# Declaring a 64-byte mask tile ahead of seven buffer groups of a two-layer attention and Fourier kernel

## The chip, the core and the metric

The kernel runs on one core of one Trainium2 chip. The metric is the device time of one execution in microseconds (us). Before the change it was 1702.32 us, the median of three runs (1701.19 to 1706.34).

## The reference

Four blocks are applied one after the other to an activation of 2048 rows by 640 columns in float32. Each block normalises its input, works on it and adds the result to it.

```python
x = x + _A_ref(_layernorm(x, axis=-1), A_wqkv, A_wo)
x = x + _B_ref(_layernorm(x, axis=-1), B_dft_seq_re, B_dft_seq_im, B_dft_hid_re, B_dft_hid_im)
x = x + _A_ref(_layernorm(x, axis=-1), A_wqkv, A_wo)
x = x + _B_ref(_layernorm(x, axis=-1), B_dft_seq_re, B_dft_seq_im, B_dft_hid_re, B_dft_hid_im)
```

Block A is local attention: 32 heads of 20 columns, and each row attends to itself and to the rows 2, 4, ... 14 above it (8 in all). Rows above the first are masked with -1e9, which is all that the mask tile of this document is for. Block B multiplies the activation by a 640 by 640 and by a 2048 by 2048 discrete Fourier matrix and keeps the real part.

## The kernel before

All matrix products run on TensorE. Each float32 operand is split into a high and a low part, held in the type float32r, and a product is three matmuls (high by high, low by high, high by low: `PASSES`, line 237). A matmul has a stationary operand of 128 by 128 that is loaded into the array (LDWEIGHTS, the rows of PEld), and a moving operand of 128 rows by up to 512 columns that streams past it. In the names of a matmul's row, `m<-r,s`, the moving operand comes first behind the arrow, and the stationary one second.

The work on TensorE, in order, is the following.

- Line 125: 18 warm-up matmuls of zeros in bfloat16, out of the tile `zero`, which has the tag s3.
- Line 381 (`qkv_mm`, block A): the projection to queries, keys and values, 128 groups of 15 matmuls with 480 moving columns. The moving operand is the split weight of one quarter of the heads, in r1_0, r1_1, r1_2 or r1_3; the stationary one is the transposed activation in s0 to s3.
- Line 531 (`wo_mm`, block A): the output projection with 320 moving columns from r2a.
- Lines 346 and 354 (`pc_pe`, `pc_sub`): transposes of 128 by 128 with the identity as the moving operand, and matmuls of 128 to 512 columns that subtract the high part again, with the negated identity `nident` as the stationary operand.
- Line 1004 (`z_mm`, block B): the first part of the sequence transform, 512 moving columns from s0 to s3 and e0 to e2, accumulated over 16 steps.
- Line 1148 (`product`, block B): the rest of the sequence transform, 512 moving columns of a split tile that rotates over zo0, zo1, e0, stg, zo2, e1, stg, ot (and pr2, pr3 in the second block B, line 1205).
- Line 1393 (`hid_mm`, block B): the hidden transform, 320 moving columns from r2a, r1_2, r1_3, pr0 to pr3 and zo3.

The attention itself (lines 450 to 511) runs on VectorE and GpSimd out of the five buffers of the tag win, which are loaded by DMA. ScalarE evicts and splits. The order of the instructions on every engine is written out by hand (a table of steps and phases, lines 868 to 902) or follows the order of the program; no queue in it depends on where a buffer lies.

Where a buffer lies in SBUF follows from the order in which the tags are first declared. The pool `sb` gives each tag, on each of the 128 partitions, as many bytes as its widest tile needs, rounded up to a multiple of 32, and puts the tags one behind the other. Lines 118 to 121 fix that order for the first of them: `zero` claims s3, and the loop of line 119 declares six more tags without using them. The mask follows with 11 float32 numbers, 44 bytes, which take 64. It is written by three memsets on GpSimd (lines 127 to 129) and read twice, each time by one copy of 11 columns to PSUM at the start of a block A (line 872).

In the built program the buffers lie as follows (bytes from the start of a partition; the remainder is that of the start divided by 256).

| buffers, in order | start before | remainder before |
|---|---|---|
| ident, nident, mhalf | 1184, 1696, 2208 | 160, 160, 160 |
| s3 | 2240 | 192 |
| r1_0 | 7360 | 192 |
| pr0 | 27840 | 192 |
| e0, e1, e2 | 32960, 38080, 43200 | 192, 192, 192 |
| win, five buffers of 3520 bytes | 48320 to 62400 | 192, 128, 64, 0, 192 |
| mask | 65920 | 128 |
| pr1, pr2, pr3, r1_1, r2a, r1_2, r1_3, zo2, zo3, ot, s0, s1, stg, zo0, s2, zo1, qs, xa, lg, xr | 65984 to 226752 | 192 each |

All slices that TensorE reads begin a multiple of 256 bytes behind the start of their buffer, so that every matmul operand has the remainder of its buffer. All tiles end at 229312 bytes.

Of the kernel before, what the change touches and what calls it, by code (L numbers as in the profile page):

```python
# [26 lines left out]
P = 128  # L27
# [55 lines left out]
SLOTS = NJ + W - 1  # L83
# [5 lines left out]
def tile_layers(ctx: ExitStack, tc: tile.TileContext, x, wqkv, wo, cs, wre, wim, out):  # L89
# [10 lines left out]
    def nm(base):  # L100
        uid[0] += 1
        return f"{base}_{uid[0]}"

    def T(shape, tag, dt=F32, bufs=1, pool=None):
        return (pool or sb).tile(shape, dt, tag=tag, name=nm(tag), bufs=bufs)
# [9 lines left out]
    nident = T([P, P], "nident", F32R)  # L115
    nc.scalar.activation(nident, ident, AF.Copy, scale=-1.0)
    mhalf = T([P, 4], "mhalf")
    zero = T([P, D], "s3", mybir.dt.bfloat16)
    for tag, w in (("r1_0", D), ("pr0", D), ("e0", 2 * D), ("e1", 2 * D), ("e2", 2 * D), ("win", SLOTS * FE)):
        T([P, w], tag, bufs=NWIN if tag == "win" else 1)  # L120
    mask = T([P, SLOTS], "mask")
    nc.vector.memset(zero, 0.0)
    wb = pt([P, 512], "m1")
    for i in range(NWARM):
# [1438 lines left out]
```

## Time and profile before

| | |
|---|---|
| median of 3 runs (lowest, highest) | 1702.32 us (1701.19, 1706.34) |
| span of the profiled execution | 1700.9 us |
| granted TensorE clock, all through | 1.00 |
| TensorE (PE) busy | 1679.7 us (99%), 8558 matmuls |
| VectorE (DVE) busy | 1339.2 us (79%) |
| ScalarE (ACT) busy | 794.0 us (47%) |
| GpSimd (POOL) busy | 625.8 us (37%) |
| DMA, share of the 16 engines in the main queue | 75.7% |

The profiled execution took 1700.9 us from its first to its last instruction; the profile lists no other time of its own for it. Busy time of TensorE is the union of its matmuls, and each of these is shown with the time that it needs to drain, so a matmul of 512 columns is listed with 389 ns while the next one begins 227 ns behind it. What a matmul costs in a stream is therefore read from the distance between starts, as the chain of waits gives it: there a piece "1.36 PE m L1148 x6" is six matmuls that took 1.36 us from the first start to the start of what follows. That chain is the work that ended last, followed back from the last instruction to what released it.

### The profile page before, as it was taken

What the parts mean: (1) busy time and instruction counts of PE and PEld (TensorE: products, weight loads), DVE (VectorE), ACT (ScalarE), POOL (GpSimd) and SP (SyncE); (2) the same over time, 40 slices, a digit from 0 to 9 for tenths busy, and PEclk for the clock granted to TensorE, in tenths of its full rate; (3) what the DMA queues carried; (4) which work ended last, traced back from release to release, by engine and by line L of the source; (5) the groups of instructions that cost most, each with busy time, mean ns of one, the idle gap of its engine ahead of it and who ended that gap; (6) DMA issues with size and microseconds to landing.
All of it is one profiled execution on the core that took longest, in us unless ns stands there. A gap on an engine that the chain in (4) does not pass through costs nothing.

```text
span 1700.9 us, 25512 instructions
## 1 busy us (share of the span) xinstructions
PE 1679.7 (99%) x8558; PEld 1464.6 (86%) x8558; DVE 1339.2 (79%) x2034; ACT 794.0 (47%) x1617; POOL 625.8 (37%) x588
## 2 busy tenths in 40 slices
PE   9999999989999999999999999999999999999999
PEld 7888988868888887899988889988888888888999
DVE  6999999978588786788639999999784656657784
ACT  5664644544354443536554335444444544444231
POOL 4899999950000000000028988999400000000000
PEclk9999999999999999999999999999999999999999
DMA  8996668857899989986377866788666776787942
GB/s 295 315 322 227 221 227 307 271 206 265 287 370 322 370 270 354 351 331 225 122 226 239 270 217 204 246 284 295 212 234 208 225 228 215 242 282 270 362 164 93
DMA packets 263139, 441.13 MB, mean 259 GB/s; under 512 B 21824, under 2 KB 126016, under 8 KB 260704
## 3 DMA queue, kind: packets, MB, share of 16 engines
q1 hardware_dynamic: 259808, 437.55, 75.7%
q10 hardware_dynamic: 3200, 1.97, 0.4%
q8 instruction: 67, 1.10, 0.3%
q14 instruction: 64, 0.52, 0.1%
HBM read 319.75 MB, written 119.67 MB: 258 GB/s over the span
## 4 chain that ended last, share of the span: by engine, by line
PE 76%; DVE 10%; POOL 6%; DMA 4%; issue 2%; ACT 0%; SPq 0%; DVEq 0%; POOLq 0%; ACTq 0%
PE m L381 19%; PE t L1148 7%; PE aux L1148 7%; PE m L1148 7%; PE pq L1148 5%; PE xt L1148 5%; PE m L1393 4%; PE aux L1393 4%; PE m L1004 3%; PE t L1004 3%; DVE pr L450 2%; PE aux L531 2%; DVE pr L490 2%; POOL pr L509 2%; PE xt L1393 2%
## 5 line engine op out<-in xcount | busy, mean ns | idle before, releaser
L381 PE MATMUL m<-r,s 128*128 128x480 f32 x1920 | 434.5, 381 | 0.6 <-ACT stg L388 0.4
L381 PEld LDWEIGHTS m<-r,s 128*128 128x128 f32 x1920 | 355.4, 188 | 53.5 <-ACT stg L388 0.8
L193 POOL TENSOR_TENSOR stats<-stats,mhalf 128x1 f32<-128x1 f32 (+1 forms) x40 | 29.2, 730 | 512.2 <-ACT stats L189 503.8
L509 POOL TENSOR_TENSOR pr<-pr 128x640 f32<-128x640 f32 x126 | 207.8, 1650 | 23.1 <-DVE pr L490 21.7
L450 DVE TENSOR_TENSOR pr<-pq,win 128x1280 f32<-128x1280 f32 x128 | 189.9, 1484 | 13.8 <-DMA win<-kvb 7.8
L490 DVE TENSOR_TENSOR pr<-pq,win 128x1280 f32<-128x1280 f32 x128 | 190.3, 1487 | 3.7 <-POOL zo L511 1.2
L453 POOL TENSOR_TENSOR pr<-pr 128x640 f32<-128x640 f32 x115 | 164.9, 1434 | 11.2 <-DVE pr L450 11.2
L460 DVE TENSOR_REDUCE lg<-pr 128x64 f32<-128x640 f32 (+1 forms) x128 | 112.7, 881 | 8.0 <-POOL pr L453 7.9
L510 POOL TENSOR_TENSOR pr<-pr 128x320 f32<-128x320 f32 x126 | 112.0, 889 | 9.9
L388 ACT COPY stg<-m 128x480 f32<-128x480 f32 x128 | 71.0, 555 | 92.9 <-PE m L381 69.1
L1004 PE MATMUL m<-s,r 128*128 128x512 f32 x366 | 111.2, 392 | 1.6 <-DMA s<-c0b 1.3
L1004 PE MATMUL t<-s,r 128*128 128x512 f32 x366 | 110.3, 390 | 0.0
L531 PE MATMUL aux<-r2a,ot 128*128 128x320 f32 x540 | 84.7, 310 | 0.7 <-ACT s L369 0.7
L531 PEld LDWEIGHTS aux<-r2a,ot 128*128 128x128 f32 x540 | 81.1, 188 | 2.8 <-ACT s L369 1.2
L1004 PEld LDWEIGHTS m<-s,r 128*128 128x128 f32 x366 | 67.6, 188 | 16.1 <-DMA s<-c0b 1.9
L1004 PEld LDWEIGHTS t<-s,r 128*128 128x128 f32 x366 | 68.7, 188 | 14.5
L1137 ACT CAST zo<-win 128x512 fp32r<-128x512 f32 x76 | 47.2, 621 | 65.4 <-PE xt L1148 30.0
L423 ACT COPY pq<-qs 128x320 f32<-128x320 f32 x64 | 27.5, 430 | 106.0 <-DVE pr L490 73.4
L1138 DVE TENSOR_TENSOR zo<-win,zo 128x512 fp32r<-128x512 f32 x76 | 52.1, 688 | 23.7 <-ACT zo L1137 23.3
L511 POOL TENSOR_TENSOR zo<-pr 128x160 f32<-128x160 f32 x126 | 67.1, 532 | 9.9
L1004 PE MATMUL xt<-s,r 128*128 128x512 f32 x183 | 68.6, 389 | 0.0
L468 ACT ACTIVATE lg<-lg 128x128 f32<-128x128 f32 x64 | 20.3, 317 | 74.6 <-DVE lg L479 74.4
(531 smaller groups left out, 3650.2 us busy)
## 6 DMA issues: line engine op xcount, KB each, us to landing
win<-cs_in SPq DMA_DIRECT2D x192, 256.0 KB, 3.8
win<-kvb SPq DMA_DIRECT2D x96, 440.0 KB, 5.3
win<-kvb SPq DMA_DIRECT2D x64, 360.0 KB, 5.0
kvb<-stg SPq DMA_DIRECT2D x60, 320.0 KB, 4.9
xa<-cs_in SPq DMA_DIRECT2D x66, 256.0 KB, 3.6
e<-cs_in SPq DMA_DIRECT2D x64, 256.0 KB, 3.9
r<-zb SPq DMA_DIRECT2D x12, 1280.0 KB, 5.9
win<-tb SPq DMA_DIRECT2D x56, 256.0 KB, 4.4
```

The source lines that it names most:

```text
L381: nc.tensor.matmul(mt[g][:, : 3 * F], st[:, a, k], wq[q][:, b, k], start=n == 0, stop=n == 14)
L388: nc.scalar.copy(sgs[q][:, :, j % 2], mt.pop(g)[:, : 3 * F].rearrange("p (a f) -> p a f", f=FE))
L450: nc.vector.tensor_tensor(pr, q, wview(u, jp, 0, [[1, FE]]), op=ALU.mult)
L453: nc.gpsimd.tensor_tensor(pv[:, :, 0:10], pv[:, :, 0:10], pv[:, :, 10:20], op=ALU.add)
L460: nc.vector.tensor_reduce(lgs[u][:, :, 2 * jp : 2 * jp + 2].rearrange("p h j w -> p (j w) h"), prq.pop((u, jp)), axis=AX.X, op=ALU.add,)
L490: nc.vector.tensor_tensor(pr.rearrange("p j w (h d) -> p j w h d", d=DH), lgs[u][:, :, 2 * jp : 2 * jp + 2].rearrange("p h j w -> p j w h" ...
L509: g.tensor_tensor(pr[:, :, 0:4], pr[:, :, 0:4], pr[:, :, 4:8], op=ALU.add)
L510: g.tensor_tensor(pr[:, :, 0:2], pr[:, :, 0:2], pr[:, :, 2:4], op=ALU.add)
L531: nc.tensor.matmul(m[:, :320], oT[(c, j)][:, a, k], wo_s["w"][:, b, k, e * 320 : (e + 1) * 320], start=(i, k) == (0, 0), stop=(i, k) == (2 ...
L1004: self.last = nc.tensor.matmul(self.z[t][k], self.xn[c][:, a, j, k * P : (k + 1) * P], self.ct[s][:, b], start=s == 0 and i == 0, stop=s = ...
L1148: nc.tensor.matmul(bank, w(a, kb), hl[b], start=start and (a, b) == (0, 0), stop=stop and (a, b) == (1, 0), skip_group_check=True,)
L1393: nc.tensor.matmul(bank[:, :320], s[:, a, k], w[:, b], start=start and (k, a, b) == (0, 0, 0), stop=stop and (k, a, b) == (KD - 1, 1, 0), ...
```

## The change

The line that declares the mask moves ahead of the first group, to directly behind `mhalf`.

```diff
     mhalf = T([P, 4], "mhalf")
+    mask = T([P, SLOTS], "mask")
     zero = T([P, D], "s3", mybir.dt.bfloat16)
     for tag, w in (("r1_0", D), ("pr0", D), ("e0", 2 * D), ("e1", 2 * D), ("e2", 2 * D), ("win", SLOTS * FE)):
         T([P, w], tag, bufs=NWIN if tag == "win" else 1)
-    mask = T([P, SLOTS], "mask")
     nc.vector.memset(zero, 0.0)
```

No instruction is added, removed or moved: the order on ScalarE and SyncE is the same word for word, and the differences on the other engines are the numbers in the names of two tiles. This is the difference on GpSimd at the start of the program, where the mask is written (with the number that a tile got when it was declared):

```order
 L126 MEMSET mhalf_73 128x4
-L127 MEMSET mask_81 128x11
+L127 MEMSET mask_74 128x11
 masks.py:199 ISA
 masks.py:199 AFFINE_SELECT ident_66<-ident_66 128x128
-L128 MEMSET mask_81 2x3
-L129 MEMSET mask_81 1x4
+L128 MEMSET mask_74 2x3
+L129 MEMSET mask_74 1x4
 L193 TENSOR_TENSOR stats_204<-stats_204,mhalf_73 128x1
```

The mask has become the 74th tile instead of the 81st, and its memsets stand where they stood. On TensorE the 18 warm-up matmuls show `s_6_75` in place of `s_5_74`, and nothing else differs.

What differs is the place of seven tags, each 64 bytes further up, and of the mask:

| buffers | start after | remainder after |
|---|---|---|
| mask | 2240 | 192 |
| s3 | 2304 | 0 |
| r1_0 | 7424 | 0 |
| pr0 | 27904 | 0 |
| e0, e1, e2 | 33024, 38144, 43264 | 0, 0, 0 |
| win, five buffers | 48384 to 62464 | 0, 192, 128, 64, 0 |

From pr1 on everything lies where it lay. In the built program 1641 of the 8558 matmuls read their moving operand from one of the six buffers s3, r1_0, pr0, e0, e1 and e2 (18 in the warm-up, 480 in line 381, 420 in line 1004, 615 in line 1148, 96 in line 1393 and 12 in line 354), 1721 read their stationary operand from one of them, and 330 read both from them. In 2702 matmuls one operand has moved and the other has not.

## The prediction

> **What bounds the kernel now.** I read the page's head first, then the waits of TensorE, then the chain of waits, stage by stage.
>
> ```profile
> span 1700.9 us, 25512 instructions
> PE 1679.7 (99%) x8558; PEld 1464.6 (86%) x8558; DVE 1339.2 (79%) x2034; ACT 794.0 (47%) x1617; POOL 625.8 (37%) x588
> PEclk9999999999999999999999999999999999999999
> ```
>
> TensorE is busy for 1679.7 of 1700.9 us at the full granted clock, so 21.2 us are all that waits can give back. The waits of TensorE, longest first and last of 23 rows, say the same:
>
> ```profile
> PE m L1004 <- ACT r L933: 2.1, 1, 2.1
> PE aux L354 <- ACT s L350: 2.0, 3, 0.9
> ...
> PE m L1004 <- DMA s<-c0b: 1.3, 2, 0.9
> ...
> PE xt L1148 <- DVE s L1311: 0.2, 1, 0.2
> ```
>
> None is over 2.1 us, and DMA has 1.3 us among them. So the time is the sum of what 8558 matmuls cost from one start to the next, and these spacings stand in the chain, where it follows TensorE without a break:
>
> ```profile
> 17.82 34.67 PE m L381 x160
> 739.56 4.40 PE t L1393 x30
> 1300.80 1.36 PE aux L1148 x6
> ```
>
> That is 34.67/160 = 216.7 ns for 480 columns, 4.40/30 = 146.7 ns for 320 and 1.36/6 = 226.7 ns for 512. From 320 to 512 columns the price rises by 80.0 ns for 192 columns, 0.417 ns each (2.4 columns per ns). What is left over is a constant: 226.7 - 213.3 = 13.3 ns for 512 columns, and 146.7 - 133.3 = 13.3 ns for 320. For 480 it is 216.7 - 200.0 = 16.7 ns. This constant is the one thing that a start address could change, because every float32r moving operand outside the transposes begins at remainder 192 today.
>
> Two stages differ in what lies close behind TensorE:
>
> ```profile
> core 0: us, PE busy (x) PEld busy (x) DVE busy (x) ACT busy (x) POOL busy (x), PEclk, DMA share, GB/s
> 100.00:200.00 100.00, 100.00 (x526) 88.75 (x525) 96.47 (x133) 60.48 (x155) 95.45 (x90) 1.00 0.75 247
> 1400.00:1500.00 100.00, 100.00 (x443) 82.81 (x442) 59.96 (x93) 43.82 (x72) 0.00 (x0) 1.00 0.75 249
> ```
>
> In block A (first row) VectorE is busy for 96.47 of 100 us and GpSimd for 95.45, so a faster TensorE would meet them at once. In block B (second row) nothing else is over 83%.
>
> **The change part by part.**
>
> *Declaration.* It adds, removes and moves no instruction and no wait; no queue is passed. The mask's three memsets and two copies of 11 columns read and write another address, and do so at two places in the whole program. Cost 0.
>
> *VectorE and ScalarE, on win and the rest.* The five win buffers rotate from the remainders 192, 128, 64, 0, 192 to 0, 192, 128, 64, 0. If the remainder mattered to these engines, reads out of win would spread wider than reads out of xa, whose two buffers both lie at 192. The views of lines 1137 and 1138, by operand (count, then minimum, median and maximum in ns):
>
> ```profile
> L1137 ACT CAST zo<-win x76: 605/622/630, 423.0 to 1564.2; 128x512 fp32r<-128x512 f32 x76
> L1137 ACT CAST zo<-xa x29: 607/622/631, 374.2 to 1553.1; 128x512 fp32r<-128x512 f32 x29
> L1138 DVE TENSOR_TENSOR zo<-win,zo x76: 679/688/694, 424.0 to 1566.2; 128x512 fp32r<-128x512 f32 x76
> L1138 DVE TENSOR_TENSOR zo<-xa,zo x29: 680/685/693, 375.7 to 1556.1; 128x512 fp32r<-128x512 f32 x29
> ```
>
> Four remainders and one give the same 622 ns and the same spread on ScalarE, and on VectorE the medians differ by 3 ns inside a spread of 15. I take 0. The outer bound is 3 ns for each of VectorE's 2034 instructions, 6.1 us either way, and they lie beside TensorE's work.
>
> *DMA.* The loads of 256 KB, 2048 bytes in a row on a partition, by where they go:
>
> ```profile
> win<-cs_in SPq DMA_DIRECT2D x192, 256.0 KB, 3.8
> xa<-cs_in SPq DMA_DIRECT2D x66, 256.0 KB, 3.6
> e<-cs_in SPq DMA_DIRECT2D x64, 256.0 KB, 3.9
> ```
>
> win, with four remainders, lands in 3.8 us, between xa and e (3.6 and 3.9 us, both at 192). Whatever a transfer gains or loses, TensorE has 1.3 us of waits for DMA to win. Bounds -1.3 to +1.3 us; I take 0.
>
> *TensorE.* 1641 matmuls get a moving operand at remainder 0 instead of 192. 18 of them are the warm-up, which leaves 1623 of float32r: 480 of 480 columns (the quarter of line 381 that uses r1_0), 1035 of 512, 96 of 320 and 12 in line 354. If the whole constant went, that would be 1623 x 13.3 = 21.6 us, and 23.2 us with the extra 3.3 ns for the 480. In the other direction, 2702 matmuls get operands of unequal remainder. Where the trace shows such a matmul already, it pays nothing for it: the subtractions of line 354 stream s at 192 past nident at 160.
>
> ```profile
> 56.29 0.23 PE xt L354
> 56.52 0.06 PE t L354
> 56.58 6.55 PE m L381 x30
> ```
>
> These are 512 and 128 columns. From 56.29 to 56.58 they take 0.29 us; 640 columns at 0.417 ns and two constants of 13.3 ns make 293 ns. So the constant is the same with unequal remainders, at least for 32 bytes of difference.
>
> Does the constant come from the remainder? The warm-up is the only other type in the trace, at the same remainder 192, out of s3:
>
> ```profile
> 4.10 2.32 PE L125 MATMUL m<-s 128*128 128x512 bf16 x10
> L125 PE MATMUL m<-s x10: 379/379/380, 4.1 to 6.0; 128*128 128x512 bf16 x10
> ```
>
> Ten matmuls of 512 columns take 2.32 us, of which the last one's duration is 0.379; (2.32 - 0.379)/9 = 215.7 ns, a constant of 2.4 ns. So remainder 192 as such does not cost 13.3 ns. The other 10.9 ns come with an operand of four bytes, either whatever its address is, or because at twice the bytes the fetch has no slack for a start in the middle of a block. The trace can't tell the two apart, since it holds no stream of long float32r matmuls at another remainder. I take the first, 0, because of the misfit of the 480 columns: a constant that came from blocks of a fixed address grid would be the same for all three lengths, which all start at 192 and are multiples of 128 bytes, yet 480 columns pay 3.3 ns more.
>
> The Trainium skill, SBUF — State Buffer, section "Specifications (TRN2)", gives 16 bytes as the line in SBUF at which an access pays for crossing; 192 and 0 are both multiples of 16, so by this rule the change gives 0, which speaks against it. No run here shows the size of that line; the rows of ScalarE above agree that steps of 64 bytes don't matter. The Trainium skill, TensorE: Matmul & The Clock Gate, section "Back-to-back issue gap", has N/2.4 + 2.5 ns for a warm matmul: the warm-up's 215.7 ns agrees with it, the 226.7 ns of float32r doesn't. If remainder 0 brought the float32r matmuls down to that formula, the change would be worth an estimated 1623 x 10.8 = 17.5 us.
>
> The sum is 0 + 0 + 0 + 0, and the profiled execution stays at 1700.9 us. It lies 1.4 us below the median of the three runs, so I forecast the median, 1702.3 us.
>
> **The rivals.**
>
> *A, faster: TensorE fetches moving operands in 128-byte blocks on a fixed grid.* Starting 64 bytes into a block, 512 columns touch 17 blocks and 320 touch 11; at 13.33 ns a block (32 columns) that is 226.7 and 146.7 ns, both as measured. At remainder 0 they would touch 16 and 10. For: two lengths of three fit to 0.1 ns, and the bfloat16 stream, with half the bytes, could hide the extra block. Against: 480 columns touch 16 blocks, 213.3 ns, and measure 216.7. Price: 21.6 us, 1702.3 - 21.6 = 1680.7 us. In block A VectorE and GpSimd are over 95% busy and may take back the 480 matmuls' 6.4 us, which leaves 1687.1. So 1679 (with the extra 1.6 us) to 1687 us.
>
> *B, slower: a matmul whose two operands lie at unequal remainders loses part of a fetch slot.* Today almost all matmuls have both at 192; afterwards 2702 don't. The smallest such loss in the rows is the 3.3 ns by which 480 columns miss the line, 2702 x 3.3 = 8.9 us, 1711.2 us; a whole constant of 13.3 ns would make 36 us, 1738 us. It decides from a loss of 5.1/2702 = 1.9 ns on. Against it stand the rows of line 354, which pay nothing at 160 against 192.
>
> *C, the remainder reaches the end through VectorE.* In block A the chain also runs over VectorE. With the 3 ns of line 1138's medians on 256 multiplications out of win (lines 450 and 490) it would be 0.8 us. That is no case of its own and lies inside the forecast.
>
> **How the numbers follow.** A measurement of this kernel can tell about 0.3%, 5.1 us, from no change, which is also the width of the three runs (1701.19 to 1706.34). The forecast, no change, has 0.74: the rows of ScalarE, VectorE, DMA and line 354, where remainders differ, show nothing. A has 0.16: its one strong witness is the fit to 17 and 11 blocks. B has 0.10: nothing in the trace shows it, and one row speaks against it. The forecast's own range is 1697 to 1708 us. That holds some 0.72, so the range reaches down into A as far as 1684 us, where about half of A lies, and not up into B, which begins at 1711. Range 1684 to 1708 us. Faster by over 0.3% 0.16, within 0.3% 0.74, slower 0.10.
>
> **What would show it.** Right: in the profile after, the chain again has 34.67 us for the 160 matmuls of line 381, 1.36 us for six of line 1148 whether they stream e0, e1 or another tile, 4.40 us for thirty of line 1393, and TensorE is busy within 5 us of 1679.7. A would show pieces of line 1148 with e as the moving operand at 1.28 us for six, and runs with r1_0 at 13 to 17 ns less per matmul. B would show more than 226.7 ns where exactly one of the two operands is in the six buffers. The forecast is wrong if the spacing differs by more than 2 ns between streams out of moved and unmoved buffers.

## The result and the profile after

The kernel became slower, by half a per cent. The kernel after takes 1711.99 us (median of 4 runs, 1710.76 to 1713.85), the kernel before 1701.76 us beside it (4 runs, 1700.83 to 1706.34); the ratio is 1.0054, with a 95% interval of 1.0041 to 1.0066. That is 10.2 us more by the medians, and 8.7 us in the two profiled executions, 1709.6 against 1700.9 us. The forecast, no change, fell, and rival B came out, near the 1711.2 us that it was given.

The head of the page of after:

```profile
span 1709.6 us, 25512 instructions
PE 1692.2 (99%) x8558; PEld 1466.5 (86%) x8558; DVE 1338.6 (78%) x2034; ACT 795.3 (47%) x1617; POOL 626.6 (37%) x588
PEclk9999999999999999999999999999999999999999
```

With the same 8558 matmuls at the same granted clock TensorE is busy for 12.5 us longer (1692.2 against 1679.7). The other engines have not moved. This is the first thing to read: the loss is inside the matmuls. TensorE's idle time was 17.4 us instead of 21.2, which is why the span rose by 8.7 us only. These are single executions, though, and the kernel with all buffers at 0 below idles for 18.2 us while its matmuls cost what they did before. So between 0.8 and 3.8 us may be waits that a slower TensorE no longer had.

The chain of waits of after, pieces of block A, then of block B, from its listing and from its windows around 1300 and 1420 us:

```profile
18.66 34.67 PE m L381 x160
...
742.96 4.40 PE t L1393 x30
...
1292.86 1.40 PE t L1148 x6
...
1316.34 1.36 PE xt L1148 x6
...
1321.78 1.39 PE m L1148 x6
...
1324.56 1.40 PE pq L1148 x6
```

Lines 381 (in this piece) and 1393 take what they took, 34.67/160 = 216.7 ns and 4.40/30 = 146.7 ns. Line 1148 had 1.36 us for every six; now some groups have 1.36 us and most others 1.38 to 1.40 us, up to 233.3 ns a matmul. The window from 1400 to 1500 us shows the same as a rate: TensorE is busy in all of it, with 437 matmuls instead of 443.

```profile
core 0: us, PE busy (x) PEld busy (x) DVE busy (x) ACT busy (x) POOL busy (x), PEclk, DMA share, GB/s
1400.00:1500.00 100.00, 100.00 (x437) 81.59 (x436) 60.25 (x92) 43.76 (x72) 0.00 (x0) 1.00 0.72 233
```

The view of line 1148 by operands (count, then minimum, median and maximum of the listed duration, which lies 162 ns above the spacing), two rows of before and then three of after:

```profile
L1148 PE MATMUL t<-e,r x204: 389/389/389, 446.6 to 1565.6; 128*128 128x512 f32 x102
...
L1148 PE MATMUL m<-stg,r x102: 389/389/389, 501.0 to 1567.0; 128*128 128x512 f32 x102
```

```profile
L1148 PE MATMUL t<-e,r x204: 387/394/398, 446.9 to 1574.1; 128*128 128x512 f32 x102
...
L1148 PE MATMUL m<-stg,r x102: 387/393/401, 502.4 to 1575.5; 128*128 128x512 f32 x102
...
L1148 PE MATMUL aux<-zo,r2a x72: 388/389/397, 494.1 to 1451.1; 128*128 128x512 f32 x72
```

Before, all three had 389 ns as their median. Streams out of e rose to 394 ns. Streams out of stg rose to 393 ns, although neither they nor their weights have moved: the 102 of this row have weights from r1_1 or r1_2. What they pay comes from what runs in front of them; 48 are among the first six matmuls behind a stream of e1 with weights at 192. Streams out of zo with weights from r2a, neither of which has moved, stay at 389 ns.

To read this by remainders, the start of each matmul in the trace is matched with the addresses of its operands in the built program. The table gives the mean distance from one start to the next, without the longest and shortest 5%:

| matmuls | moving, stationary at | count | before, ns | after, ns |
|---|---|---|---|---|
| line 1148, 512 columns | 192, 192 | 1551 | 226.7 | 229.4 |
| | 0, 192 | 513 | 226.7 | 231.5 |
| | 192, 0 | 426 | 226.7 | 233.1 |
| | 0, 0 | 102 | 226.7 | 230.2 |
| line 1004, 512 columns | 192, 192 | 390 | 227.1 | 229.3 |
| | 0, 192 | 330 | 227.4 | 230.8 |
| | 192, 0 | 150 | 227.4 | 233.5 |
| line 381, 480 columns | 0, 192 | 360 | 217.0 | 218.5 |
| | 192, 0 | 360 | 216.9 | 216.5 |
| line 1393, 320 columns | 0, 192 and 192, 0 | 546 | 146.7 | 146.5 |

So 512 columns pay 3 to 6 ns more where the remainders differ, 480 columns 1.5 ns in one case and nothing in the other, 320 columns nothing. Matmuls whose two remainders are equal pay some 3 ns too; those are mostly the ones behind an unequal one. One passage of line 1148, at 554 us, reads 236, 231, 235 ns for three matmuls at 192 and 0, and then 229, 232, 231, 227, 226, 227 ns for equal ones. Three equal ones is the least after which a steady 226 to 227 ns came back in line 1148; behind some streams of e it took ten. A change of both remainders at once costs something too, without any unequal pair: at 501.0 us a steady stretch at 192 and 192 is followed by six matmuls at 0 and 0, with 228, 229, 234, 235, 225, 231 ns.

The other terms of the prediction stand. DMA, then ScalarE by operand:

```profile
win<-cs_in SPq DMA_DIRECT2D x192, 256.0 KB, 4.1
xa<-cs_in SPq DMA_DIRECT2D x66, 256.0 KB, 4.0
e<-cs_in SPq DMA_DIRECT2D x64, 256.0 KB, 4.0
```

```profile
L1137 ACT CAST zo<-win x76: 604/621/628, 422.3 to 1571.8; 128x512 fp32r<-128x512 f32 x76
L1137 ACT CAST zo<-xa x29: 606/621/632, 374.0 to 1560.6; 128x512 fp32r<-128x512 f32 x29
```

win lands as xa and e do, and ScalarE reads both in 621 ns. VectorE is busy for 1338.6 us, against 1339.2.

### The profile page after: what moved, and what is told of

Read it like the earlier page. It is cut to its first block, busy times and chain, and to the rows that moved or that the text cites. A ratio compares the mean times of both kernels' runs of the same rounds, so it can differ in the third digit from the quotient of the medians.

```text
span 1709.6 us, 25512 instructions
## 1 busy us (share of the span) xinstructions
PE 1692.2 (99%) x8558; PEld 1466.5 (86%) x8558; DVE 1338.6 (78%) x2034; ACT 795.3 (47%) x1617; POOL 626.6 (37%) x588
## 4 chain that ended last, share of the span: by engine, by line
PE 82%; DVE 6%; DMA 5%; POOL 4%; issue 2%; ACT 1%; SPq 0%; DVEq 0%; ACTq 0%; POOLq 0%
PE m L381 20%; PE aux L1148 7%; PE t L1148 7%; PE m L1148 7%; PE pq L1148 5%; PE xt L1148 5%; PE aux L531 5%; PE m L1004 4%; PE t L1004 4%; PE m L1393 4%; PE aux L1393 3%; PE xt L1004 2%; PE xt L1393 2%; PE pq L1393 2%; PE t L1393 2%
## 5 line engine op out<-in xcount | busy, mean ns | idle before, releaser
L381 PEld LDWEIGHTS m<-r,s 128*128 128x128 f32 x1920 | 355.8, 188 | 53.3 <-ACT r L653 1.2
```

Of the source, the lines that this page charges most:

```text
L381: nc.tensor.matmul(mt[g][:, : 3 * F], st[:, a, k], wq[q][:, b, k], start=n == 0, stop=n == 14)
```

## The experiments

The **pair theory** is that a float32r matmul pays where its moving and its stationary operand lie at different remainders of 256 bytes. Its rivals: the value 0 itself costs (**value theory**); the cost comes from going between remainders from one matmul to the next (**transition theory**); the cost comes from win's new remainders and not from TensorE's operands.

In most kernels here every tag is declared ahead of its use, so that its place in the memory is chosen by the order of a list; the instructions stay as they are. The helper shifts the line numbers by 9 to 11 (line 1148 becomes 1157, 1158 or 1159). "Distance" is the start of the moving operand less that of the stationary one, modulo 256. One edit is shown in full, of the others the list.

### All buffers of TensorE at 0

```diff
+    ORDER = (
+        ("mask", 11, 1), ("s3", 1280, 1), ("r1_0", 5120, 1), ("pr0", 1280, 1), ("e0", 1280, 1),
+        ("e1", 1280, 1), ("e2", 1280, 1), ("pr1", 1280, 1), ("pr2", 1280, 1), ("pr3", 1280, 1),
+        ("r1_1", 5120, 1), ("r2a", 6400, 1), ("r1_2", 5120, 1), ("r1_3", 5120, 1), ("zo2", 1280, 1),
+        ("zo3", 1280, 1), ("ot", 1280, 1), ("s0", 1280, 1), ("s1", 1280, 1), ("stg", 1024, 2),
+        ("zo0", 1280, 1), ("s2", 1280, 1), ("zo1", 1280, 1), ("xa", 640, 2), ("xr", 640, 1), ("win", 880, 5),
+    )
+    for tag, w, n in ORDER:
+        if tag == "mask":
+            mask = T([P, SLOTS], "mask")
+        else:
+            T([P, w], tag, bufs=n)
     zero = T([P, D], "s3", mybir.dt.bfloat16)
-    for tag, w in (("r1_0", D), ("pr0", D), ("e0", 2 * D), ("e1", 2 * D), ("e2", 2 * D), ("win", SLOTS * FE)):
-        T([P, w], tag, bufs=NWIN if tag == "win" else 1)
-    mask = T([P, SLOTS], "mask")
```

> All buffers that TensorE streams or loads (except the two identities) begin at remainder 0; the five win buffers keep the remainders of the changed kernel (0, 192, 128, 64, 0). Pair theory (a matmul pays when its two operands have unequal remainders, nothing for the value itself): 512 columns are back at 226.7 ns throughout, and the time is that of before, 1702 us within 4 us. Value theory (remainder 0 is itself the slow one): every matmul now lies there, so more than the changed kernel's 10 us, 1715 us or over. Win or DMA theory (the shifted win buffers or the transfers cost the 10 us): 1712 us, as the changed kernel.

Measured: 1702.59 us, ratio to before 1.0006 (0.9995 to 1.0016). TensorE is busy for 1680.9 us of a span of 1699.1 us, and the chain is back at 1.36 us for six:

```profile
1300.55 1.36 PE t L1157 x6
```

win lies at the same remainders as in the kernel after and every moving operand outside the transposes at 0, and nothing is lost. The value theory and win fall. This is also the change carried to its end, all six buffers and the rest at multiples of 256 bytes: it is worth nothing either way.

### Constant distances in line 1148: +64, 128, -32

In these the tags that line 1148 streams (zo0 to zo2, e0, e1, stg, ot, pr2, pr3) lie at one remainder and almost all others at another, so line 1148 has one distance throughout and no transition. For +64:

```diff
+        ("mask", 11, 1), ("zo0", 1280, 1), ("zo1", 1280, 1), ("zo2", 1280, 1), ("e0", 1280, 1),
+        ("e1", 1280, 1), ("stg", 1024, 2), ("ot", 1280, 1), ("pr2", 1280, 1), ("pr3", 1280, 1),
+        ("win", 880, 5), ("s3", 1280, 1), ("r1_0", 5120, 1), ("pr0", 1280, 1), ("e2", 1280, 1),
...
```

> The nine tags that line 1148 streams (zo0, zo1, zo2, e0, e1, stg, ot, pr2, pr3) at remainder 0, all others at 192: in line 1148 every one of the 2592 matmuls has unequal remainders, and the moving remainder never changes from one to the next. Pair theory: all of line 1148 at about 233 ns, 2592 x 6.7 ns = 17 us, 1719 us in all. Transition theory (what costs is the change of remainder from one matmul to the next, the next few then run late): line 1148 at 226.7 ns, 1702 to 1704 us.

For 128, mhalf, the mask and 32 bytes of padding stand between the two sets:

```diff
+        ("stg", 1024, 2), ("ot", 1280, 1), ("pr2", 1280, 1), ("pr3", 1280, 1), ("mhalf", 4, 1),
+        ("mask", 11, 1), ("pad11", 8, 1), ("s3", 1280, 1), ("r1_0", 5120, 1), ("pr0", 1280, 1),
...
```

> The same nine tags 128 bytes apart from the others (remainders 160 and 32). Pair theory, if any unequal remainder costs the same: line 1148 at about 233 ns, 1719 us. If the cost follows a grid of 128 bytes: 226.7 ns and 1702 us. If the distance decides where two streams collide, a spacing under 226.7 ns is possible as well, down to 215.8 ns, which would be 28 us less, 1674 us. Transition theory: 1702 to 1704 us.

For -32, only the padding:

```diff
+        ("stg", 1024, 2), ("ot", 1280, 1), ("pr2", 1280, 1), ("pr3", 1280, 1), ("pad9", 8, 1),
+        ("s3", 1280, 1), ("r1_0", 5120, 1), ("pr0", 1280, 1), ("e2", 1280, 1), ("pr1", 1280, 1),
...
```

> The same nine tags 32 bytes apart from the others (remainders 192 and 224). Pair theory, any unequal remainder: 1719 us with line 1148 at about 233 ns; with a cost that grows with the distance: about half of that, 1710 us. A grid of 64 bytes: 1702 us. Transition theory: 1702 to 1704 us.

Measured, with the mean start to start in line 1148:

| distance | time, us | ratio to before | TensorE busy, us | line 1148, ns |
|---|---|---|---|---|
| 0 (all at 0) | 1702.59 | 1.0006 (0.9995 to 1.0016) | 1680.9 | 226.7 |
| +64 | 1709.57 | 1.0042 (1.0027 to 1.0057) | 1689.2 | 229.0 |
| 128 | 1716.11 | 1.0084 (1.0067 to 1.0101) | 1694.0 | 232.2 |
| -32 | 1717.00 | 1.0086 (1.0069 to 1.0103) | 1699.3 | 233.4 |

The groups of line 1148 by operand, of -32 (line 1158), and the chain of the same kernel:

```profile
L1158 PE MATMUL t<-e,r 128*128 128x512 f32 x204 | 53.1, 396 | 0.0
```

```profile
1302.75 1.40 PE t L1158 x6
```

At -32 every such piece of the second block B has 1.40 us: 233.3 ns, without a break and without any transition. The transition theory falls as the account of the whole; what is left of it is the cost of equal matmuls behind unequal ones, and behind a change of both remainders (about 0.7 us of line 1148 in the kernel after). The pair theory stands for the rest. Its size was off at +64, where the spacing repeats 226, 229, 232 ns and the mean is 229.0 and not 233 ns.

### Is it the size or the sign of the distance?

Three sets now differ, so that lines 1148, 1004 and 381 each have a distance of their own. The first set holds r1_0 to r1_3, r2a, xr, zo3, pr0 and pr1, the second the streams of line 1148, the third s0 to s3 and e2; what lies between them sets the distances (mhalf 32 bytes, mask 64, win 192 modulo 256).

```diff
+        ("xr", 640, 1), ("zo3", 1280, 1), ("pr0", 1280, 1), ("pr1", 1280, 1), ("mhalf", 4, 1),
+        ("zo0", 1280, 1), ("zo1", 1280, 1), ("zo2", 1280, 1), ("e0", 1280, 1), ("e1", 1280, 1),
+        ("stg", 1024, 2), ("ot", 1280, 1), ("pr2", 1280, 1), ("pr3", 1280, 1), ("mask", 11, 1),
+        ("s0", 1280, 1), ("s1", 1280, 1), ("s2", 1280, 1), ("s3", 1280, 1), ("e2", 1280, 1), ("xa", 640, 2),
...
```

> Distance = remainder of the moving operand minus that of the stationary one. Line 1148 at +32, line 1004 at +96, line 381 at -96. So far 512 columns cost 226.7 ns at 0, 229.0 at +64, 232.4 at 128, 233.3 at -32. If only the size of the distance counts, line 1148 is at 233.3 ns and the time near 1719 us; if its sign counts as well (two streams that run one behind the other), +32 may be anywhere from 226.7 ns down, 1702 us or less, to 233.

The second order has the third set ahead of the second, `mhalf, s0..s3, e2, mask, zo0..pr3`:

> Line 1148 at +96, line 1004 at +32, line 381 at -32. By the size of the distance: line 1004 at 233.3 ns (6 us more in all), line 1148 between the 229.0 of 64 and the 232.4 of 128, 1710 to 1722 us. By a signed law: line 1004 here equals line 1148 of the run at +32, and line 1148 here equals line 1004 of that run, since it is the distance alone that decides.

The third has win in the first gap and mhalf in the second, `win, zo0..pr3, mhalf, s0..s3, e2`:

> Line 1148 at -64, line 1004 at -32, line 381 at +32. By the size of the distance: line 1148 at 229.0 ns, as at +64, and 1709 us plus 6 us for line 1004 at 233.3. By a signed law: line 1148 at about 233 ns, as the streams at -64 in the changed kernel had it, 1717 us plus 6.

One run of each, beside 1703.89 us for one of the kernel before (2520 of the 2592 matmuls of line 1148 have the distance named, 72 another):

| order | time, us | line 1148: distance, ns | line 1004: distance, ns | line 381: distance, ns |
|---|---|---|---|---|
| first | 1721.59 | +32, 233.4 | +96, 233.5 | -96, 217.3 |
| second | 1722.77 | +96, 233.3 | +32, 233.4 | -32, 218.4 |
| third | 1723.48 | -64, 233.4 | -32, 233.3 | +32, 219.2 |

Line 1148 has 233.4 ns at -64 and had 229.0 at +64, so the size alone doesn't decide there, and the third order came out as the signed law had it. Beyond that neither size nor sign orders the costs of 512 columns: +32, -32, +96 and -64 all end at 233.3 to 233.5 ns. At 480 columns an unequal pair costs 0.3 to 2.2 ns over the 217.0 of before.

### Every distance, by itself

A block of 39 trains of 30 matmuls on zeros, 36 of float32r and 3 of bfloat16, runs ahead of the work, between the warm-up and line 381. Within a float32r train the moving operand (out of r2a) and the stationary one (out of r1_1) keep one distance, one length and one width of the weights, and rotate through several tiles a multiple of 256 bytes apart; the bfloat16 trains read the tile of the warm-up. The added lines move the work's own by 35 and lengthen the span to 1951.8 us.

```diff
+    def p_dist(d, n=512, c=P, v=0):
+        for i in range(30):
+            a, b = ((0, 0), (0, 1), (1, 0))[i % 3]
+            m0, w0 = 1024 * b + (d + v) // 4, 1024 * a + 128 * (i // 3 % 4) + v // 4
+            nc.tensor.matmul(
+                wb[:c, :n], pw[:, w0 : w0 + c], pm[:, m0 : m0 + n], start=i == 0, stop=i == 29, skip_group_check=True
+            )
...
+        for d in (0, 4, 8, 16, 24, 32, 48, 64, 80, 96, 112, 128, 160, 192, 224, 240, 256, 512):
+            p_dist(d)
...
```

> The kernel before with a block of matmuls of zeros ahead of its work, 30 of each kind in one bank: 512 float32r columns at 18 distances between the moving and the stationary operand (0, 4, 8, 16, 24, 32, 48, 64, 80, 96, 112, 128, 160, 192, 224, 240, 256, 512 bytes), then 256 to 496 columns at the distances 0 and 32, loads of 64 and 32 columns at both, both operands shifted together by 32 and 64, and bfloat16 at 0, 32 and 64. The block adds some 330 us, which is not a cost of any layout. Pair theory: 226.7 ns at 0, 256 and 512 and with both shifted together, 233 at 32, 229 at 64, 232 at 128, and 146.7 for 320 columns at either distance. If some distance under 32 lets the streams pass, a spacing between 215.8 and 226.7 shows there. If what the load takes from the stream is the cost, loads of 64 and 32 columns in a uniform run bring the spacing toward 216; if not, they leave it. Bfloat16, with half the bytes: 215.8 at all three.

The chain of waits in windows of single trains: distance 32, distance 256, 320 columns at distance 0 and then at 32, both operands shifted together by 32, and bfloat16 (line 142) at 0:

```profile
42.80 7.00 PE m L135 x30
...
119.66 6.83 PE m L135 x30
...
136.99 4.38 PE m L135 x30
...
169.54 4.37 PE m L135 x30
...
226.12 6.82 PE m L135 x30
...
240.01 6.27 PE m L142 x29
```

At 32 bytes 30 matmuls take 7.00 us, 233.3 ns each. At 256 bytes, and with both shifted, they take 6.82 to 6.83 us, and that holds a settling of some 0.02 us at the train's start. 320 columns don't differ. The means from start to start over the settled part of each train (the 9th to the 28th matmul):

| train | ns |
|---|---|
| 512 columns, distance 0, 256, 512; both shifted by 32 or by 64 | 226.7 |
| distance 80, 112 | 230.9, 230.8 |
| distance 16, 128 | 231.7, 232.4 |
| distance 8, 24, 32, 48, 64, 96, 192, 224, 240 | 233.3 to 233.5 |
| distance 160, 4 | 234.3, 236.7 |
| distance 0, weights of 64 or 32 columns | 229.6, 231.7 |
| distance 32, weights of 64 or 32 columns | 230.9, 226.7 |
| distance 0: 256, 320, 384, 448, 480, 496 columns | 120.0, 146.7, 173.4, 206.7, 216.7, 223.4 |
| distance 32: the same | 117.9, 146.7, 173.4, 206.7, 220.0, 224.5 |
| bfloat16, 512 columns, distance 0, 32, 64 | 215.9 each |

Distances of 256 and 512 bytes cost what 0 costs, and 0 is the cheapest of the 16 remainders tried. At 512 columns an unequal pair pays 4 to 10 ns. At the other lengths 32 is the only distance tried: there 480 columns pay 3.3 ns, 496 pay 1, and 320 to 448 nothing (256 gain 2). The 229 ns expected at a distance of 64 didn't come: a train by itself has 233.4.

### Shorter loads of the weights

In the two low passes of line 1148 (now 1149), two of every three matmuls, half the weights' columns are loaded, at distance 0:

```diff
+                    n = P if (a, b) == (0, 0) else 64
...
-                        bank,
-                        w(a, kb),
+                        bank[:n],
+                        w(a, kb)[:, :n],
```

> Buffers as before. In line 1148 the two low passes of each product load 64 stationary columns instead of 128 and write 64 rows of the bank, so half of the low corrections are left out; the moving streams stay at 512 columns. If the constant of 13.3 ns is what the load of the next weights takes from the stream, a matmul beside which 64 columns are loaded costs about 220 ns instead of 226.7, two of three: 1728 x 6.7 ns = 11.5 us less, 1690 us. If the constant belongs to float32r or to the stream alone, 226.7 ns and 1702 us.

One run: 1708.11 us beside 1703.89 us. The two forms of one group stand apart:

```profile
L1149 PE MATMUL t<-e,r 128*64 128x512 f32 x136 | 42.3, 392 | 0.0
L1149 PE MATMUL t<-e,r 128*128 128x512 f32 x68 | 26.5, 390 | 0.0
```

In the kernel before this group had 389 ns. With half the load 392 ns are listed, and with the full load behind it 390; from start to start the line has a mean of 229.4 ns, 2.7 more than before, and not less. So the constant of 13.3 ns is not time that the load takes in proportion to its columns. In the trains above, too, narrower weights move 512 columns between 226.7 and 233.3 ns. Narrower weights also mean that fewer rows of the bank are written, and no run here separates the two.

### The change in two parts

r1_0 alone moved, and the other five alone:

```diff
+        ("mask", 11, 1), ("r1_0", 5120, 1), ("win", 880, 5), ("s3", 1280, 1), ("pr0", 1280, 1),
+        ("e0", 1280, 1), ("e1", 1280, 1), ("e2", 1280, 1), ("pr1", 1280, 1), ("pr2", 1280, 1),
...
```

> One part of the change: r1_0 alone moves to remainder 0 (win takes the remainders 0, 192, 128, 64, 0; s3, pr0, e0 to e2 stay at 192). Pair theory, from the steady spacings measured so far: 672 matmuls of 512 columns at -64, 6.6 ns each, 4.4 us; 480 of line 381 at +64, 1.5 ns each, 0.7 us; 336 equal ones within four places behind an unequal one, about 4 ns each, 1.3 us. Together 6.4 us, 1708 us. If the weights' buffer didn't matter and only the streamed buffers did: 1702 to 1703 us.

```diff
+        ("mask", 11, 1), ("s3", 1280, 1), ("pr0", 1280, 1), ("e0", 1280, 1), ("e1", 1280, 1), ("e2", 1280, 1),
+        ("win", 880, 5), ("r1_0", 5120, 1), ("pr1", 1280, 1), ("pr2", 1280, 1), ("pr3", 1280, 1),
...
```

> The other part: s3, pr0, e0, e1 and e2 at remainder 0, r1_0 stays at 192. Pair theory: 1023 matmuls of 512 columns at +64, 2.3 ns each in a steady run and up to 4.8 between others, 2.4 to 4.9 us; 84 at -64, 0.6 us; 480 of line 381 at -64, -0.3 us; 618 equal ones behind them, about 4 ns each, 2.5 us. Together 5 to 8 us, 1707 to 1710 us.

Measured beside 1703.39 us: r1_0 alone 1706.01 us, 1.0017 (1.0008 to 1.0027); the others 1710.20 us, 1.0041 (1.0026 to 1.0056). That is 2.9 and 7.0 us by the ratios, 9.9 together, against 9.2 for the whole by its ratio. Line 1148 with e, in r1_0 alone and in the others alone:

```profile
L1157 PE MATMUL t<-e,r x204: 389/389/398, 444.4 to 1566.1; 128*128 128x512 f32 x102
```

```profile
L1157 PE MATMUL t<-e,r x204: 388/394/398, 447.4 to 1573.0; 128*128 128x512 f32 x102
```

The others alone ended within the 5 to 8 us expected. With r1_0 alone the expectation of 6.4 us was too high. Its matmuls cost what they were to (192 against 0: 233.6 ns in line 1148 and 233.4 in line 1004), and TensorE is busy for 1684.5 us, 4.8 more than before; but the equal neighbours stayed at 227.1 ns. The span of its profiled execution, 1701.3 us, is no measure of the loss: that execution was the fastest of the ten. Where the rest of the 4.8 us went, beyond the 2.9 us of the runs, is not shown. Most of what equal matmuls lose in line 1148 (229.6 ns with the others alone) comes with the moved streams, which are e0 and e1 there.

## Why the prediction was wrong, and where it was right

**The part that held.** The kernel is the sum of its matmuls' spacings; VectorE, ScalarE, DMA, win and the mask's own five instructions count for nothing, in after and in the kernel with all buffers at 0. Rival B named the right condition, and its proof ahead: more than 226.7 ns where exactly one operand has moved. That what is lost is "part of a fetch slot" is not shown.

**The step that failed** is in the part on TensorE: "So the constant is the same with unequal remainders, at least for 32 bytes of difference", read from 0.29 us of two matmuls of line 354. Those rows hold what an unequal pair costs elsewhere. The 512 columns of this line lie at distance 32 in the kernel before as well, and the view of line 354 of before shows them longer than the 389 ns of line 1148:

```profile
L354 PE MATMUL xt<-s,nident x24: 392/398/500, 56.1 to 1058.7; 128*128 128x512 f32 x24
```

Start to start, 23 of the 24 take 230 to 237 ns, as an unequal pair does; the train at distance 32 has 233.3. (No run puts the two operands of line 354 at one remainder, so for this line itself the cause is inferred.) The 128 columns behind them take 55 to 60 ns, 2 to 7 ns over 53.3. The sum of the two was compared with two constants of 13.3 ns: 7 ns too much in one matmul and some 9 ns too little in the other gave 292 for 293. The length of 128 columns was outside the lengths from which the constant had been read, and its row ended the one rival that had the right condition. That is why B had a chance of 0.10 only.

**"I take the first, 0, because of the misfit of the 480 columns"** was right on the value of the remainder (all at 0 is worth nothing, so A's blocks on a fixed grid are refuted), but it put the question to the moving operand alone. What matters is where the two operands stand to each other. The Trainium skill, SBUF — State Buffer, section "Specifications (TRN2)", had been weighed with its line of 16 bytes; distances of 16, 32 and 64 bytes cost 5 to 7 ns in these trains and distances of 256 and 512 nothing, so for this pair the measurement decides.

**B's size** was nearly right as a sum by luck, for its terms were wrong. It put 3.3 ns on 2702 matmuls, 8.9 us; measured are 9.2 us by the ratio and 10.2 by the medians. By the table of after the terms are, in us: 513 x 4.8 + 426 x 6.4 = 5.2 on the unequal ones of line 1148, 330 x 3.4 + 150 x 6.1 = 2.0 on those of line 1004, 1551 x 2.7 + 102 x 3.5 = 4.5 on equal ones of line 1148 and some 1.0 on those of line 1004, and about 0.4 on line 381: 13.1, against 12.5 us more of busy time. The 1419 unequal matmuls of 512 columns paid more than 3.3 ns each, the 546 of line 1393 nothing and the 720 of line 381 little. The term for the equal neighbours, behind unequal pairs and behind changes of both remainders, was in no case of the prediction, nor was the part, 0.8 to 3.8 us, that less waiting may give back; the two have opposite signs.

**What stays open.** Which resource the two operands share was not shown. The Trainium skill, TensorE: Matmul & The Clock Gate, section "Step-by-step: what each phase is for", gives TensorE two independent read ports for the stream and the weights, so that loading the next weights takes nothing from the running matmul. In these runs the place of the weights changes a float32r stream by up to 10 ns, so that the weights are not without effect on it; whether that happens at a port is not shown. A meeting of the load with the running stream is one explanation, but is only argued, and the trace speaks against its simplest form. It lists the load of the next weights 2 to 4 ns behind the start of the running matmul, so those would be the weights that the stream meets. With r1_0 alone, however, matmuls of line 1148 whose own weights lie at 0 and the next ones at 192 take 233.4 ns, and those whose own lie at 192 and the next ones at 0 take 225.9 (76 of each, all streams at 192). With the others alone the first matmul of e behind a steady stretch takes 236.6 ns at once (37 cases), although its weights were loaded beside a stream at their own remainder. So the cost goes with the matmul's own pair. Nor is it known why +64 costs 2.3 ns in line 1148 and 6.7 ns in a train by itself, or why the constant at distance 0 is 13.3 ns for 256 to 384 and for 512 columns but 16.7 to 20 ns for 448 to 496.

## What to carry to other kernels

Keep every buffer that TensorE reads in float32r matmuls of 480 columns or more at one remainder of 256 bytes; which one made no difference here (192 before, 0 with all moved), so align all or none, and put small odd-sized tiles ahead of or behind the whole set. Where TensorE is the bound, compare its busy time beside the span: with the same cost per matmul, idle time was 21.2 us in one execution and 18.2 in another. And before a row is taken as proof that an effect is absent, read each of its matmuls by itself and against its own length.

## What the runs showed of the hardware

- A float32r stream of 512 columns takes 226.7 ns where its operands start at the same remainder of 256 bytes, and 230.8 to 236.7 ns at 15 other distances from 4 to 240 bytes; bfloat16 takes 215.9 ns at the three distances tried.
- After unequal pairs, three equal ones at the least, and ten behind some streams of e, passed in line 1148 of the kernel after before a steady 226 to 227 ns came back.
- A change of both remainders at once, from 192 and 192 to 0 and 0, gave 228, 229, 234, 235, 225 and 231 ns.
- The cost goes with the matmul's own two operands: with r1_0 alone, 233.4 ns where the own weights differ and the next don't, 225.9 ns where the next differ and the own don't.
- Narrower weights can slow the stream: at distance 0, weights of 128, 64 and 32 columns give 226.7, 229.6 and 231.7 ns; at distance 32 they give 233.3, 230.9 and 226.7 ns.
- No layout tried beats the one before; the best are the two with distance 0 in every matmul outside the transposes and line 354.
